# Attention by two head pairs per pipeline step, with the softmax sums' 1e-9 on GpSimd

## The chip, the cores and the metric

The kernel runs on one core of one Trainium2 chip. TensorE (PE) multiplies and transposes, VectorE (DVE), ScalarE (ACT) and GpSimd (POOL) work on vectors, and SyncE (SP) issues most of the DMAs. The metric is the device time of the core in microseconds (us), as the median of the runs shown.

## The reference

Three computations follow each other:

```
attention   q, k, v: 4 x 8 heads x 768 x 64; a key is kept if it is one of the first 8, or at most 95 behind
            scores = q k / 8 - slope[h] * distance, kept keys only; a = exp(scores - max)
            a = a / (sum(a) + 1e-9);  x = a v, as 3072 tokens x 512
experts     logits = x w_gate (512 x 8); each token goes to its best expert, with its softmax value as gate
            out = gate * (relu(x w1[e]) w2[e]),  w1 512 x 1024, w2 1024 x 512
feed-forward  h = out w_in (512 x 2048); g = (a0 + a1 h + a2 h^2 + a3 h^3) / (1 + |b0||h| + |b1| h^2 + 1e-6)
            result = g w_out (2048 x 512)
```

## The kernel before

Attention works on units: a unit is a tile of 128 tokens, 24 in all (4 sequences of NI = 6 tiles), and in each unit on NP = 4 pairs of heads. `seq` lists the 96 steps (u, hp), and the loop over t runs one step of it at a time as a software pipeline of four stages. Step t first issues stage D of step t-5, then A of step t, C of step t-3 and B of step t-1:

- A (stA, L586; stA2, L600 and L604): S = q k for the two heads of a pair, six products in two PSUM banks `sj` (q and k are split in two float32r parts, so three products a head). On VectorE a fused add and minimum takes the negated, masked scores to `nn` and their minimum `mn` (L600, shown as CUSTOM_DVE_ANT_0, and as ISA in the order). On ScalarE the exponential gives `pp` and its row sums `sm` (L604). A window has 232 keys, or 128 in a sequence's first tile.
- B (stB): four transpositions on TensorE (L616, `pt`), the 1e-9 added to the two sums on VectorE (L619, `rs`), `pt` copied to `pT` (on ScalarE for pair 1, L622, on VectorE for the others, L624), and the reciprocal of `rs` (L626).
- C (stC): four products with v (L638, in bank `ps_o`), a copy to `oT` on ScalarE (L641).
- D (stD): one product of `oT` with `iw`, which holds a unit matrix and the gate's weights (L647, in bank `ps_ox`). So x comes back with tokens on the partitions, and beside it the pair's part of the logits. VectorE multiplies both by `rs` (x L653, lw L657). After the last pair of a unit the logits are summed (lg, L666) and x is stored.

The same engines do other work in the loop. emit_tstep transposes q and k of later units (L512), copies them to `raw` on ScalarE (L520, L523, L524) and subtracts on GpSimd (L525), one half at a time. Every second unit from unit 5 on a block of expert 0's weights is loaded, and split a unit later: ScalarE rounds (L314), GpSimd subtracts (L315). Routing runs in small steps that wait in `filler`; each call of fill() between two larger operations emits one. Units are routed in groups of 4, 7, 6, 3, 3 and 1; a group's steps end with the sorted positions `pos` (L215), a store of the gates (L198) and one indirect DMA a unit on GpSimd that scatters token numbers to `tid` (L136, behind a memset, L135).

When all groups but the last two are routed, SyncE reads the numbers of expert 0's first 256 tokens back from DRAM (L128, `eidx`), and GpSimd gathers these tokens' rows of x (L250, `raw`). They form the early tile. Its products with expert 0's weights go in 64 small steps of three matmuls (L267 to L269), each step followed by work for ScalarE and VectorE (hh L293, hl L294). They fill what the attention leaves of TensorE at its end.

After the loop the string TAILS orders what is left: B, C and D with a number are these stages of the step that many from the end, G is the scaling of the gathered rows on VectorE (L254), X their transposition (L260), F with a number so many routing steps, E so many steps of the early tile. Then all engines meet a branch on `slow` (L821, L822; not taken here), TensorE counts the tokens (L1237), VectorE plans the experts' tiles (L1239 to L1378 and on), the early tile's remaining steps run, a second branch follows (L1445), and the experts begin. Each engine executes its own instructions in the order in which they are emitted.

## Time and profile before

| | us |
|---|---|
| median of 3 runs | 1171.92 |
| lowest and highest | 1169.7, 1175.31 |
| span of the profiled execution | 1169.0 |
| busy in it: PE, DVE, ACT, POOL | 1109.0, 954.6, 760.1, 434.6 |

The three runs lie around the span of the profiled execution, the median 2.9 us above it. Busy times of an engine overlap those of the others. The attention loop takes up roughly the first 265 us of the span, the tail and the first branch go to 289 us, the early tile's rest to 316 us, the experts and the feed-forward part to the end.

### The profile page before, as it was taken

Reading aid. Unit: us, or ns where it says so; the run is one execution under the profiler, and the core shown is the slowest. Engines: PE = TensorE matmul, PEld = TensorE weight load, DVE = VectorE, ACT = ScalarE, POOL = GpSimd, SP = SyncE. Lnnn points to the kernel's source line nnn. Section 1 sums busy time; section 2 is a strip of 40 time slices with the busy share of each in tenths; the row PEclk is TensorE's granted clock in tenths of the full one; section 3 lists DMA queues with packets and bytes.
Section 4 is the critical chain, followed back from the end, with each engine's and each line's share of the span. In section 5 each row is a group of like instructions: output and inputs, shape, how many; then the busy total and the mean of one; then the engine's idle time right before and its main releaser. Section 6 shows DMA issues by size and latency. Waiting matters only on the chain.

```text
span 1169.0 us, 19466 instructions
## 1 busy us (share of the span) xinstructions
PE 1109.0 (95%) x6636; PEld 982.8 (84%) x6636; DVE 954.6 (82%) x2200; ACT 760.1 (65%) x1695; POOL 434.6 (37%) x454
## 2 busy tenths in 40 slices
PE   8998988987699999999997999999999999999997
PEld 7876776766699888999996888999999999999996
DVE  7897878774667967887667999989898998989985
ACT  5886777662254555554555777777777777777774
POOL 4253444532422323132114535344342535344342
PEclk9998989798799999999999999999999999999999
DMA  9887787403477877887663000000100000000000
GB/s 177 186 132 162 164 94 173 87 20 105 114 226 251 302 243 248 283 302 269 211 204 123 1 27 28 28 28 1 46 10 28 28 27 28 19 27 10 1 28 27
DMA packets 122820, 130.65 MB, mean 112 GB/s; under 512 B 62799, under 2 KB 92671, under 8 KB 122704
## 3 DMA queue, kind: packets, MB, share of 16 engines
q1 hardware_dynamic: 108416, 99.78, 32.7%
q0 software_dynamic: 8624, 22.48, 5.6%
q10 hardware_dynamic: 5664, 6.98, 1.6%
q8 instruction: 56, 0.92, 0.4%
q14 instruction: 60, 0.49, 0.2%
HBM read 99.60 MB, written 29.61 MB: 111 GB/s over the span
## 4 chain that ended last, share of the span: by engine, by line
PE 59%; DVE 7%; ACT 2%; issue 2%; DMA 2%; POOL 1%; ACTq 0%; POOLq 0%; DVEq 0%; SPq 0%
PE acc L268 10%; PE acc L267 10%; PE acc L269 10%; PE ph L267 7%; PE ph L268 7%; PE ph L269 7%; PE ps_t L267 3%; PE ps_t L269 3%; PE ps_t L268 3%; DVE ta L1546 1%; DVE tcc L1545 1%; DVE ta L1595 1%; PE ps_t L260 1%; DVE tcc L1605 1%; DMA ysT<-y 1%
## 5 line engine op out<-in xcount | busy, mean ns | idle before, releaser
L1560 POOL TENSOR_TENSOR gl<-tcc,gh 128x384 fp32r<-128x384 f32 x127 | 128.9, 1015 | 293.8 <-ACT gh L1554 229.1
L267 PE MATMUL acc<-wa_h,gh 128*128 128x512 f32 x384 | 150.2, 391 | 5.9 <-ACT gh L1554 4.3
L269 PE MATMUL acc<-wa_h,gl 128*128 128x512 f32 x384 | 151.4, 394 | 1.7 <-POOL gl L1560 1.7
L268 PE MATMUL acc<-wa_l,gh 128*128 128x512 f32 x384 | 151.3, 394 | 0.0
L1545 DVE SCALAR_TENSOR_TENSOR tcc<-tcc,cf,tb 128x384 f32<-128x384 f32 x128 | 117.9, 921 | 13.7 <-DVE tcc L1605 0.5
L1596 ACT ACTIVATE tb<-ta,cf 128x384 f32<-128x384 f32 x128 | 79.0, 617 | 42.8 <-DVE ta L1595 32.8
L1595 DVE SCALAR_TENSOR_TENSOR ta<-ta,cf,tb 128x384 f32<-128x384 f32 x128 | 81.4, 636 | 31.0 <-ACT tb L1590 29.7
L604 ACT ACTIVATE pp<-nn,mn 128x232 f32<-128x232 f32 (+1 forms) x192 | 88.8, 465 | 26.6 <-DVE mn L600 23.5
L1546 DVE SCALAR_TENSOR_TENSOR ta<-ta,cf,tb 128x384 f32<-128x384 f32 x128 | 103.3, 807 | 0.0
L269 PEld LDWEIGHTS acc<-wa_h,gl 128*128 128x128 f32 x384 | 72.1, 188 | 20.0 <-POOL gl L1560 4.7
L267 PE MATMUL ph<-xh,wb_h 128*128 128x384 f32 (+3 forms) x252 | 86.8, 344 | 1.7 <-DVE tcc L1605 1.2
L267 PEld LDWEIGHTS acc<-wa_h,gh 128*128 128x128 f32 x384 | 72.1, 188 | 19.0 <-ACT gh L1554 5.7
L268 PE MATMUL ph<-xl,wb_h 128*128 128x384 f32 (+3 forms) x252 | 86.3, 343 | 0.3 <-DVE xl L953 0.2
L269 PE MATMUL ph<-xh,wb_l 128*128 128x384 f32 (+3 forms) x252 | 86.1, 342 | 0.0
L268 PEld LDWEIGHTS acc<-wa_l,gh 128*128 128x128 f32 x384 | 72.0, 188 | 11.4
L616 PE MATMUL pt<-ident,pp 128*116 128x128 f32 (+1 forms) x384 | 71.6, 311 | 2.3 <-ACT pp L604 2.3
L1589 ACT ACTIVATE ta<-ph 128x384 f32<-128x384 f32 x78 | 38.1, 488 | 54.0 <-PE ph L269 54.0
L600 DVE CUSTOM_DVE_ANT_0 nn<-sj,bm 128x232 f32<-128x232 f32 (+1 forms) x192 | 65.8, 373 | 6.8 <-PE sj L586 4.7
L1551 DVE SCALAR_TENSOR_TENSOR tcc<-ta,tcc 128x384 f32<-128x384 f32 x128 | 70.4, 550 | 0.0
L616 PEld LDWEIGHTS pt<-ident,pp 128*116 128x116 f32 (+1 forms) x384 | 49.3, 185 | 20.9 <-issue 15.3
L1554 ACT ACTIVATE gh<-tcc 128x384 fp32r<-128x384 f32 x128 | 65.1, 509 | 2.3 <-DVE tcc L1551 2.3
L1601 ACT ACTIVATE tb<-tb 128x384 f32<-128x384 f32 x128 | 65.1, 509 | 0.0
(335 smaller groups left out, 3352.9 us busy)
## 6 DMA issues: line engine op xcount, KB each, us to landing
wst<-in_moe_w_dram SPq DMA_DIRECT2D x72, 512.0 KB
wst<-in_moe_w_in_dram SPq DMA_DIRECT2D x16, 512.0 KB
wst<-in_moe_w_out_dram SPq DMA_DIRECT2D x16, 512.0 KB
xs<-x SPq DMA_DIRECT2D x24, 256.0 KB
hh<-in_v_dram SPq DMA_DIRECT2D x17, 256.0 KB
wf_in<-cv POOLq DMA_DIRECT2D x16, 256.0 KB
wf_out<-cv POOLq DMA_DIRECT2D x16, 256.0 KB
wst<-wf_in SPq DMA_DIRECT2D x8, 512.0 KB
```

The costliest lines, as they stand in the source:

```text
L267: nc.tensor.matmul(ps, lh, rh, start=first, stop=False)
L268: nc.tensor.matmul(ps, lh, rl, start=False, stop=False)
L269: nc.tensor.matmul(ps, ll, rh, start=False, stop=last)
L600: nc.vector.tensor_tensor_reduce(nn[:, 0:w], s2[j][:, 0:w], bmh, op0=ALU.add, op1=ALU.min, scale=1.0, scalar=3.0e38, accum_out=mn)
L604: nc.scalar.activation(pp[:, 0:w], nn[:, 0:w], AF.Exp, scale=-1.0, bias=mn, accum_out=sm[:, j:j + 1])
L616: nc.tensor.transpose(pt[0:w2, j, r, :], pv[:, r, :], ident)
L1545: nc.vector.scalar_tensor_tensor(pc_, pc_, na0, pb_, op0=ALU.add, op1=ALU.mult)
L1546: nc.vector.scalar_tensor_tensor(pa_, pa_, one, pb_, op0=ALU.add, op1=ALU.mult)
L1551: nc.vector.scalar_tensor_tensor(pc_, pa_, -2.0, pc_, op0=ALU.add, op1=ALU.mult)
L1560: eng.tensor_tensor(gl, prev[2], gh.bitcast(F32), op=ALU.subtract)
L1595: nc.vector.scalar_tensor_tensor(ta, ta, b1, tb, op0=ALU.mult, op1=ALU.add)
L1596: nc.scalar.activation(tb, ta, AF.Ln, bias=one)
```

## The change

A step of the pipeline now handles a group of HG = 2 pairs, so that a unit has two steps and the loop 48. The lags become 1 step for B, 2 for C and 3 for D. S of both pairs goes to the same two banks, the second pair 256 columns further on. The four transpositions, the products with v and the product with `iw` are issued for both pairs one after the other; `ps_o` and `ps_ox` hold both pairs, and one instruction each copies `oT` (256 columns), multiplies x (256) and lw (32). The reciprocal is taken once for four sums and moves to stage C; the 1e-9 is added on GpSimd, once for four sums. A step has 11 calls of fill() (before, 7), two halves of emit_tstep (one), and the warming products, mask pieces and TAILS are rewritten for 48 steps. Comments are gone, so lines of the attention part have other numbers after the change: S L588, the reduction L604, the exponential L608, the add L617, the transpositions L624, pT L631 and L633, C L647, oT L650, the reciprocal L651, D L659, x L667, lw L671, lg L680. In the diff, what builds the loads, stores and splits inside the loop is left out; they keep their conditions, with hg in place of hp.

```diff
-TAILS = "D5 G F1 C3 C2 B1 X0 C1 F3 D4 X1 D3 F3 F7 F1 E2 D2 F2 F1 E2 F2 F2 F1 F3 E1 F5 D1"
+TAILS = "D3 G F1 C2 B1 X0 C1 F3 D2 X1 F3 F7 F1 E2 D1 F2 F1 E2 F2 F2 F1 F3 E1 F5"
-WARM2 = 2, 2, 2, 4
+WARM2 = 4, 6
-MS = (7, 2, 4, 2)
+MS = (7, 2, 4, 4)
...
-        seq = [(u, hp) for u in range(units) for hp in range(NP)]
+        HG = 2
+        NG2 = NP // HG
+        seq = [(u, hg) for u in range(units) for hg in range(NG2)]
...
-        def stA(u, hp):
+        def stA(u, hg):
             bb, i = divmod(u, NI)
             w = P if i == 0 else WIN
-            s2 = []
             k1 = (i + 1) * GK
-            for j in range(2):
-                sj = psS.tile([P, 512], F32, name="sj")
-                s2.append(sj)
-            for n, (x, y) in enumerate(((0, 0), (0, 1), (1, 0))):
-                for j in range(2):
-                    hd = slice(j * D, (j + 1) * D)
-                    nc.tensor.matmul(s2[j][:, 0:w], qT[u][x][hd, hp, :], kr[hd, y, hp, k1 - w:k1], start=n == 0, stop=n == 2)
-            st[u, hp] = s2
-        def stA2(u, hp):
+            s2 = [psS.tile([P, 512], F32, name="sj") for j in range(2)]
+            for a in range(HG):
+                hp = HG * hg + a
+                for n, (x, y) in enumerate(((0, 0), (0, 1), (1, 0))):
+                    for j in range(2):
+                        hd = slice(j * D, (j + 1) * D)
+                        nc.tensor.matmul(s2[j][:, a * 256:a * 256 + w], qT[u][x][hd, hp, :], kr[hd, y, hp, k1 - w:k1],
+                                         start=n == 0, stop=n == 2)
+            st[u, hg] = s2
+        def stA2(u, hg):
             i = u % NI
             w = P if i == 0 else WIN
-            s2 = st[u, hp]
-            sm = wk.tile([P, 2], F32, name="sm", bufs=5)
-            pr = []
+            s2 = st[u, hg]
+            sm = wk.tile([P, HG, 2], F32, name="sm", bufs=4)
+            pr = {}
             for j in range(2):
-                h = 2 * hp + j
-                nn = wk.tile([P, WIN], F32, name=f"nn{j}")
-                mn = wk.tile([P, 1], F32, name=f"mn{j}")
-                bmh = bm[:, h, WIN:WB] if i == 0 else bm[:, h, 0:WIN]
-                nc.vector.tensor_tensor_reduce(nn[:, 0:w], s2[j][:, 0:w], bmh, op0=ALU.add, op1=ALU.min,
-                                               scale=1.0, scalar=3.0e38, accum_out=mn)
-                fill()
-                pp = wk.tile([P, WIN], F32, name=f"pp{j}")
-                nc.scalar.activation(pp[:, 0:w], nn[:, 0:w], AF.Exp, scale=-1.0, bias=mn, accum_out=sm[:, j:j + 1])
-                pr.append(pp)
-            st[u, hp] = [pr, sm]
-        def stB(u, hp):
+                for a in range(HG):
+                    h = 2 * (HG * hg + a) + j
+                    nn = wk.tile([P, WIN], F32, name="nn", bufs=4)
+                    mn = wk.tile([P, 1], F32, name="mn", bufs=6)
+                    bmh = bm[:, h, WIN:WB] if i == 0 else bm[:, h, 0:WIN]
+                    nc.vector.tensor_tensor_reduce(nn[:, 0:w], s2[j][:, a * 256:a * 256 + w], bmh, op0=ALU.add,
+                                                   op1=ALU.min, scale=1.0, scalar=3.0e38, accum_out=mn)
+                    fill()
+                    pp = wk.tile([P, WIN], F32, name=f"pp{a}{j}", bufs=2)
+                    nc.scalar.activation(pp[:, 0:w], nn[:, 0:w], AF.Exp, scale=-1.0, bias=mn, accum_out=sm[:, a, j:j + 1])
+                    pr[a, j] = pp
+            st[u, hg] = [pr, sm]
+        def stB(u, hg):
             i = u % NI
             w2 = P // 2 if i == 0 else HWIN
-            pr, sm = st[u, hp]
-            pt = psT.tile([P, 2, 2, P], F32, name="pt")
-            for j in range(2):
-                pv = pr[j][:, 0:2 * w2].rearrange("p (c r) -> p r c", r=2)
-                for r in range(2):
-                    nc.tensor.transpose(pt[0:w2, j, r, :], pv[:, r, :], ident)
-            pT = wk.tile([HWIN, 2, 2, P], F32, name="pT", bufs=3)
-            rs = wk.tile([P, 2], F32, name="rs", bufs=7)
-            nc.vector.tensor_scalar(rs, sm, 1e-9, None, op0=ALU.add)
-            fill()
-            if hp in ONACT:
-                nc.scalar.activation(pT[0:w2], pt[0:w2], AF.Copy)
-            else:
-                nc.vector.tensor_copy(pT[0:w2], pt[0:w2])
-            fill()
-            nc.vector.reciprocal(rs, rs)
-            fill()
-            st[u, hp] = [pT, rs]
-        def stC(u, hp):
+            pr, sm = st[u, hg]
+            rs = wk.tile([P, HG, 2], F32, name="rs", bufs=5)
+            nc.gpsimd.tensor_scalar(rs, sm, 1e-9, None, op0=ALU.add)
+            pts = []
+            for a in range(HG):
+                pt = psT.tile([P, 2, 2, P], F32, name="pt")
+                for j in range(2):
+                    pv = pr[a, j][:, 0:2 * w2].rearrange("p (c r) -> p r c", r=2)
+                    for r in range(2):
+                        nc.tensor.transpose(pt[0:w2, j, r, :], pv[:, r, :], ident)
+                pts.append(pt)
+            pTs = []
+            for a in range(HG):
+                pT = wk.tile([HWIN, 2, 2, P], F32, name="pT", bufs=3)
+                fill()
+                if HG * hg + a in ONACT:
+                    nc.scalar.activation(pT[0:w2], pts[a][0:w2], AF.Copy)
+                else:
+                    nc.vector.tensor_copy(pT[0:w2], pts[a][0:w2])
+                pTs.append(pT)
+                fill()
+            st[u, hg] = [pTs, rs]
+        def stC(u, hg):
             i = u % NI
             w2 = P // 2 if i == 0 else HWIN
-            pT, rs = st[u, hp]
+            pTs, rs = st[u, hg]
             vt = vts[u]
             ox = psM.tile([P, 512], F32, name="ps_o")
-            for r in range(2):
-                for j in range(2):
-                    nc.tensor.matmul(ox[j * D:(j + 1) * D, 0:P], vt[0:w2, 2 * hp + j, r, :], pT[0:w2, j, r, :],
-                                     start=(r == 0), stop=(r == 1))
-            oT = wk.tile([P, P], F32, name="oT", bufs=4)
-            nc.scalar.activation(oT, ox[:, 0:P], AF.Copy)
-            st[u, hp] = [oT, rs]
-        def stD(u, hp):
-            oT, rs = st.pop((u, hp))
+            for a in range(HG):
+                for r in range(2):
+                    for j in range(2):
+                        nc.tensor.matmul(ox[j * D:(j + 1) * D, a * P:(a + 1) * P], vt[0:w2, 2 * (HG * hg + a) + j, r, :],
+                                         pTs[a][0:w2, j, r, :], start=(r == 0), stop=(r == 1))
+            oT = wk.tile([P, HG, P], F32, name="oT", bufs=2)
+            nc.scalar.activation(oT, ox[:, 0:HG * P].rearrange("p (a q) -> p a q", a=HG), AF.Copy)
+            nc.vector.reciprocal(rs, rs)
+            st[u, hg] = [oT, rs]
+        def stD(u, hg):
+            oT, rs = st.pop((u, hg))
             ox = psM.tile([P, 512], F32, name="ps_ox")
-            nc.tensor.matmul(ox[:, 0:P + 2 * E], oT, iw[:, hp, :], start=True, stop=True)
-            if hp == 0:
+            OW = P + 2 * E
+            for a in range(HG):
+                nc.tensor.matmul(ox[:, a * OW:(a + 1) * OW], oT[:, a, :], iw[:, HG * hg + a, :], start=True, stop=True)
+            if hg == 0:
                 x = wk.tile([P, DM], F32, name="x", bufs=2)
                 lw = wk.tile([P, H, E], F32, name="lw", bufs=2)
                 xt[u] = (x, lw)
             x, lw = xt[u]
-            nc.vector.tensor_tensor(x[:, hp * P:(hp + 1) * P].rearrange("p (j d) -> p j d", j=2),
-                                    ox[:, 0:P].rearrange("p (j d) -> p j d", j=2),
-                                    rs.unsqueeze(2).to_broadcast([P, 2, D]), op=ALU.mult)
+            ov = ox[:, 0:HG * OW].rearrange("p (a c) -> p a c", a=HG)
+            xw = HG * P
+            nc.vector.tensor_tensor(x[:, hg * xw:(hg + 1) * xw].rearrange("p (a j d) -> p a j d", a=HG, j=2),
+                                    ov[:, :, 0:P].rearrange("p a (j d) -> p a j d", j=2),
+                                    rs.unsqueeze(3).to_broadcast([P, HG, 2, D]), op=ALU.mult)
             fill()
-            nc.vector.tensor_tensor(lw[:, 2 * hp:2 * hp + 2, :],
-                                    ox[:, P:P + 2 * E].rearrange("p (j e) -> p j e", j=2),
-                                    rs.unsqueeze(2).to_broadcast([P, 2, E]), op=ALU.mult)
-            if hp == NP - 1:
+            nc.vector.tensor_tensor(lw[:, 2 * HG * hg:2 * HG * (hg + 1), :].rearrange("p (a j) e -> p a j e", a=HG),
+                                    ov[:, :, P:OW].rearrange("p a (j e) -> p a j e", j=2),
+                                    rs.unsqueeze(3).to_broadcast([P, HG, 2, E]), op=ALU.mult)
+            if hg == NG2 - 1:
...
-            if 0 <= t - 5 < L:
-                stD(*seq[t - 5])
+            if t >= 3:
+                stD(*seq[t - 3])
-                stC(*seq[t - 3])
+            if t >= 2:
+                stC(*seq[t - 2])
...
-            if nxt:
-                emit_tstep(*nxt.pop(0))
+            for _ in range(3 if t == 0 else 2):
+                if nxt:
+                    emit_tstep(*nxt.pop(0))
...
             fill(True)
+            fill(True)
```

TensorE in one step in the middle of the loop, in the order of issue, before; `sj` are the scores' banks, `pt` the transposed probabilities:

```order
L647 MATMUL ps_ox<-iw,oT 128x144
L586 MATMUL sj<-kr,qh 128x232 x4
L586 MATMUL sj<-kr,ql 128x232 x2
L638 MATMUL ps_o<-pT,hh 64x128 x4
L616 MATMUL pt<-ident,pp_1755 116x128 x2
L616 MATMUL pt<-ident,pp_1760 116x128 x2
L512 MATMUL ps_qk<-ident,hl 128x128 x2
```

and after:

```order
L659 MATMUL ps_ox<-iw,oT 128x144 x2
L588 MATMUL sj<-kr,qh 128x232 x4
L588 MATMUL sj<-kr,ql 128x232 x2
L588 MATMUL sj<-kr,qh 128x232 x4
L588 MATMUL sj<-kr,ql 128x232 x2
L647 MATMUL ps_o<-pT,hh 64x128 x8
L624 MATMUL pt<-ident,pp_1666 116x128 x2
L624 MATMUL pt<-ident,pp_1676 116x128 x2
L624 MATMUL pt<-ident,pp_1671 116x128 x2
L624 MATMUL pt<-ident,pp_1681 116x128 x2
L512 MATMUL ps_qk<-ident,xh 128x128 x4
```

The five kinds of products that followed each other once for each pair now follow once for two pairs, each with twice the number.

GpSimd near the end of the loop, before; `kr` and `ql` are the low parts of k and q, `tid` the scattered token numbers, `raw` the gathered rows:

```order
L525 TENSOR_TENSOR kr<-raw,kr 128x4x128
L525 TENSOR_TENSOR ql<-raw,qh 128x512
L198 DMA xs<-g_4620 128x3x16
L525 TENSOR_TENSOR kr<-raw,kr 128x4x128
L135 MEMSET nop 1x1
L136 DMA tid<-tok,pos 24704x1
L135 MEMSET nop 1x1
L136 DMA tid<-tok,pos 24704x1
L135 MEMSET nop 1x1
L136 DMA tid<-tok,pos 24704x1
L525 TENSOR_TENSOR ql<-raw,qh 128x512
L250 DMA raw<-xs,eidx 128x528 x2
```

and after:

```order
L617 TENSOR_SCALAR rs<-sm 128x4
L198 DMA xs<-g_4293 128x3x16
L617 TENSOR_SCALAR rs<-sm 128x4
L135 MEMSET nop 1x1
L136 DMA tid<-tok,pos 24704x1
L135 MEMSET nop 1x1
L136 DMA tid<-tok,pos 24704x1
L135 MEMSET nop 1x1
L136 DMA tid<-tok,pos 24704x1
L617 TENSOR_SCALAR rs<-sm 128x4
L250 DMA raw<-xs,eidx 128x528 x2
L617 TENSOR_SCALAR rs<-sm 128x4
```

The three scatters of tiles 17 to 19 stood between subtractions of q and k, which the loop issues for later units; they now come behind the last of these, between the adds of the last steps, and the add of the last step comes behind the two gathers.

VectorE just ahead of the first branch (its last two rows), before; `hl` is the low part of the early tile's hidden values, `pos` the last tile's position:

```order
L294 SCALAR_TENSOR_TENSOR hl<-sj,hh 128x256
L206 TENSOR_TENSOR rr<-sj,oh 128x8
L190 TENSOR_SCALAR se<-se 128x1
L209 TENSOR_SCALAR em_5146<-em_5146 128x1
L193 RECIPROCAL gate<-se 128x1
L294 SCALAR_TENSOR_TENSOR hl<-sj,hh 128x256
L212 TENSOR_REDUCE rank<-rr 128x1
L197 COPY g_5204<-gate 128x16
L215 TENSOR_TENSOR pos<-em_5146,rank 128x1
L294 SCALAR_TENSOR_TENSOR hl<-sj,hh 128x256 x2
L821 TENSOR_LOAD slow
L822 COMPARE_AND_BRANCH
```

and after:

```order
L206 TENSOR_TENSOR rr<-sj,oh 128x8
L190 TENSOR_SCALAR se<-se 128x1
L209 TENSOR_SCALAR em_4553<-em_4553 128x1
L294 SCALAR_TENSOR_TENSOR hl<-sj,hh 128x256
L193 RECIPROCAL gate<-se 128x1
L212 TENSOR_REDUCE rank<-rr 128x1
L197 COPY g_4578<-gate 128x16
L215 TENSOR_TENSOR pos<-em_4553,rank 128x1
L294 SCALAR_TENSOR_TENSOR hl<-sj,hh 128x256
L834 TENSOR_LOAD slow
L835 COMPARE_AND_BRANCH
```

Of the six rows that write `hl` ahead of the branch, two are left, and the rest comes behind the branch.

## Rows read from the trace of the kernel before

**Rows 1.** The top of the page: span, busy time of each engine.

```profile
span 1169.0 us, 19466 instructions
...
PE 1109.0 (95%) x6636; PEld 982.8 (84%) x6636; DVE 954.6 (82%) x2200; ACT 760.1 (65%) x1695; POOL 434.6 (37%) x454
```

**Rows 2.** Windows: stretch, us, busy PE, PEld, DVE, ACT, POOL; granted clock, DMA share, GB/s.

```profile
23.00:92.00 69.00, 64.31 (x639) 51.40 (x638) 58.79 (x287) 54.73 (x183) 26.64 (x25) 1.00 0.88 164
92.00:102.00 10.00, 9.40 (x62) 7.25 (x63) 7.92 (x35) 6.78 (x22) 4.28 (x3) 0.66 1.19 240
...
282.00:318.00 36.00, 19.39 (x127) 19.00 (x127) 18.31 (x65) 6.61 (x13) 10.17 (x8) 0.76 0.35 85
...
318.00:1169.00 851.00, 833.52 (x4264) 759.94 (x4264) 711.51 (x1080) 561.04 (x1059) 307.64 (x301) 1.00 0.31 105
```

**Rows 3.** Timeline of TensorE, one pair step: start us, us, engine, line, tiles.

```profile
42.57 0.41 PE L647 MATMUL ps_ox<-iw,oT 128*128 128x144 f32 x2
...
42.91 0.49 PE L586 MATMUL sj<-kr,qh 64*128 64x232 f32 x4
...
43.43 0.66 PE L638 MATMUL ps_o<-pT,hh 116*64 116x128 f32 x8
...
44.02 0.70 PE L616 MATMUL pt<-ident,pp 128*116 128x128 f32 x4
...
44.78 0.41 PE L647 MATMUL ps_ox<-iw,oT 128*128 128x144 f32 x2
```

**Rows 4.** Timeline of TensorE, windows that cut the merged rows of the same step.

```profile
43.12 0.27 PE L586 MATMUL sj<-kr,qh 64*128 64x232 f32 x2
...
43.81 0.28 PE L638 MATMUL ps_o<-pT,hh 116*64 116x128 f32 x2
```

**Rows 5.** Timeline of TensorE: first S products of pair 6 and of pair 94.

```profile
22.98 0.48 PE L586 MATMUL sj<-kr,qh 64*128 64x232 f32 x4
...
260.44 0.49 PE L586 MATMUL sj<-kr,qh 64*128 64x232 f32 x4
```

**Rows 6.** Waits, 92 to 102 us: engine line <- releaser, us, times, longest.

```profile
DVE x L653 <- DMA xs<-x: 3.7, 1, 3.7
```

**Rows 7.** The add: its durations ns min/median/max; its group at 23 to 263 us.

```profile
L619 DVE TENSOR_SCALAR rs<-sm x96: 115/164/2454, 15.8 to 267.9; 128x2 f32<-128x2 f32 x96
...
L619 DVE TENSOR_SCALAR rs<-sm 128x2 f32<-128x2 f32 x90 | 44.9, 499 | 0.0
```

**Rows 8.** Timeline of VectorE at 40 and 199 us.

```profile
40.10 1.13 DVE L619 TENSOR_SCALAR rs<-sm 128x2 f32<-128x2 f32 x1
...
199.06 2.31 DVE L184 TENSOR_TENSOR cum<-cum,oh 128x8 bf16<-128x8 bf16 x1
```

**Rows 9.** Timeline of GpSimd at 40 and 199 us.

```profile
39.93 1.28 POOL L525 TENSOR_TENSOR kr<-raw,kr 128x512 fp32r<-128x512 f32 x1 [2.66 <-ACT kr L524]
...
199.01 2.35 POOL L315 TENSOR_TENSOR wa_l<-wst,wa_h 128x1024 fp32r<-128x1024 f32 x1 [1.75 <-ACT wa_h L314]
```

**Rows 10.** Timeline of GpSimd, 240 to 296 us.

```profile
250.42 0.96 POOL L136 DMA_INDIRECT tid<-tok,pos  x1 [0.22 <-issue]
...
262.48 0.98 POOL L250 DMA_INDIRECT raw<-xs,eidx  x1 [9.68 <-issue]
...
281.10 0.98 POOL L136 DMA_INDIRECT tid<-tok,pos  x1 [0.22 <-issue]
```

**Rows 11.** Waits of SP's queue, 250 to 300 us.

```profile
SPq L128 <- DMA tid<-tok,pos: 10.2, 1, 10.2
```

**Rows 12.** Timeline of VectorE in the tail and behind the branch.

```profile
266.99 0.87 DVE L254 TENSOR_SCALAR raw<-raw 128x512 f32<-128x512 f32 x2
...
296.20 6.77 DVE L1378 SCALAR_TENSOR_TENSOR svals<-tot,redo 128x1 int32<-128x1 f32 x1
```

**Rows 13.** Timeline of TensorE: early tile, and the first expert product.

```profile
303.35 0.58 PE L268 MATMUL ph<-hl,wa_h 128*128 128x256 f32 x1 [7.68 <-DVE hl L294]
...
317.86 0.47 PE L267 MATMUL ph<-wa_h,cv 128*128 128x512 f32 x1 [2.10 <-ACT nop L1445]
```

56 lines of the change are left out of this document (26 added, 30 removed).

## The prediction

> **What bounds the kernel now.** I began with the page's top [rows 1]: one core, a span of 1169.0 us, TensorE busy 95% of it. An average like that hides stages, so next came the windows [rows 2]. From 318 us to the end TensorE is busy 833.52 of 851 us: the expert and feed-forward products fill it, the change touches nothing there, and that part only shifts. All that the change can move lies before 318 us: the attention loop (to about 265 us), a tail, a branch and the early tile of expert 0. In the stretch 23 to 92 us TensorE is busy 64.31 of 69 us, VectorE 58.79, ScalarE 54.73.
>
> Then the timeline of TensorE inside one undisturbed pair step [rows 3]: the product of stage D starts at 42.57 and again at 44.78 us, 2.21 us later, with no idle time named in between. TensorE sets the step. But it does not stream all that time. Cutting the window inside the merged rows [rows 4] shows single starts: products of one shape follow each other after about 0.11 us, and at a change of shape more time goes by. D's two slots from 42.57 to the first S product at 42.91 take 0.34, 0.12 over; 42.91 to the second S slot at 43.12 is 0.21; from there to C at 43.43 is 0.31 for two slots, so 0.20 in the last; C's first slot has 0.05 more than 0.11 (43.43 to 43.81 for three); the last C at 43.81 to the first transposition at 44.02 is 0.21; and the six 128x128 products from 44.02 to 44.78 take 0.76, 0.10 more than six times 0.11. The excesses 0.12, 0.10, 0.09, 0.05, 0.10 and 0.10 make 0.56 us a step that is spent on changing over.
>
> The loop as a whole is slower than its step. Pair 6 starts S at 22.98, pair 94 at 260.44 [rows 5]: 237.5 us for 88 steps, against 88 x 2.21 = 194.5. The missing 43 us I divided by walking the gaps between S starts and asking what each gap's last wait was: about 18 us hang on DMA, the first and largest at 92 us, where VectorE waits 3.7 us for a store of x to drain and TensorE's products for it in turn [rows 6]; about 25 us hang on bursts of VectorE and the half-speed stretch that follows one of them. What feeds those bursts is in rows 7: the 1e-9 add, 128x2 elements, takes 0.164 us in the median and 2.454 at most, 44.9 us over 90 of them, so about 30 us more than 90 x 0.164. The long ones lie under GpSimd work: 1.13 us at 40.10 [rows 8] while GpSimd runs its 1.28 us subtraction from 39.93 [rows 9].
>
> The Trainium skill, "SBUF — State Buffer", section "SBUF: two separate sides", says that VectorE and GpSimd share one port pair as an exclusive lock. The trace agrees with it: the add ends as the GpSimd subtraction does. By that page the routing's steps with two SBUF inputs stay exposed after the change, and rows 8 and 9 show one, 2.31 us at 199.06 under GpSimd's weight split from 199.01. By the page the sum below stays as it is; were the lock only the add's, it would be 6 us lower.
>
> **The change, part by part.** *Grouping.* Streaming stays; the changes of shape come once for two pairs. A group step has the floor 2 x 2.21 - 0.56 = 3.86 us for TensorE in place of 4.42. ScalarE is next: 54.73 us over some 30 pairs [rows 2] is 1.8 us a pair, 3.6 a group, and one merged copy of o saves under 0.1; VectorE, less some 10 us of the adds' excess in that stretch (a third of 30), has 1.63 a pair and, without the adds themselves, 3.1 a group. Three engines at 80 to 95% of 3.86 don't run at the floor. I take 3.97; bounds are 3.86 and 4.42 (nothing gained). 44 groups at 3.97 are 175 us.
>
> *Lag.* D runs three group steps behind A, where it was five pair steps, and C two where it was three; in time the lags grow from 11.1 to 11.9 us and 6.6 to 7.9. So chains have as much time as before and I cost it at zero. Two pairs in one bank means that the first reduction waits until the second pair's products of that bank are there as well, about 0.5 us later. The cover is VectorE's own slack, 3.86 less 3.1; if routing steps fill that, each such group loses up to 0.5. The Trainium skill, "PSUM — Partial Sum Buffer", section "PSUM bank collisions raise a hardware error", forbids an engine to read a bank while TensorE writes it, which would make this wait hard. No run here shows a collision; by the page the sum stays, as the 0.5 is counted.
>
> *The add and the reciprocal.* 96 adds leave VectorE: 96 x 0.164 at most (they overlap their neighbours in part), plus the 30 us of excess. 48 adds of 128x4 come to GpSimd. The trace has no such operation there; its nearest rows are VectorE's own add, at least 0.115 us [rows 7], and GpSimd's 1.28 us for a 128x512 subtraction [rows 9], I take 0.2 for its size, 10 us in all on an engine that is 37% busy [rows 1]. It can be late, though: it stands behind the subtractions and, every fourth step, behind the weight split of 2.35 us. The reciprocal that waits for it is emitted a group step later, so it has some 3.9 us; I cost it at zero, with 0 and 2 us for each of some ten splits and scatters as bounds.
>
> *Stalls after.* Most of VectorE's 25 us go; the routing's own exposure stays, I leave 6. The DMA's 18 us don't go: they come where loads, stores and the scatters of token numbers fall together, the DMA share stands at 1.19 at 92 to 102 us [rows 2], and a faster loop asks for the same bytes sooner. I take 22, bounds 14 and 35. So the last group step starts at about 23 + 175 + 6 + 22 = 226 us, where the last two pairs began at 260.44: 34 us gained, bounds 20 and 44.
>
> *The tail.* Here the change costs. Routing steps are dealt out by fill() slots, 28 a unit before and 22 now, so the group of tiles 17 to 19 gets its positions later in the loop. Before, its third scatter started at 250.42, 10 us ahead of pair 94. Now its three scatters stand behind the add of group 45, in the last group step. What follows has a fixed length: SP waits 10.2 us for the scattered numbers [rows 11], GpSimd gathers the early tile's rows from 262.48 [rows 10], VectorE scales them at 266.99 [rows 12]. From the end of the third scatter (251.4) to that is 15.6 us; before, the loop's last steps covered all of it, and VectorE reached the scaling without waiting. Now the scatters end about 2.8 us into the last group step, the scaling comes at 226 + 2.8 + 15.6 = 244.4, VectorE reaches it some 5 us into that step, and everything queued behind it there (the last copies of pT, x and the last routing) stands for 13 us. The add of the last group also stands behind both gathers. From the scaling to the end of the last scatter it was 15.1 us (to 282.1, rows 10); with D only twice and fewer early products in between I take 13.5. The last scatter then ends 32 us after the last group step's start, before it was 21.6 after pair 94's. Loss: 10 us, bounds 4 and 14.
>
> *Behind the branch.* Before the branch 8 steps of the early tile's products are emitted in place of 24; the order shows two rows that write hl there where six stood. The 16 steps go behind the branch. TensorE spends 19.39 us on some 42 steps in 282 to 318 us [rows 2], 0.46 each at the mixed clock (0.76): 16 x 0.46 = 7 us later. The 7.68 us that TensorE waits at 303.35 [rows 13], behind one VectorE operation of 6.77 us at 296.20 [rows 12], I leave as they are. Bounds: 0 (the branch comes sooner relative to the landing of the scatters, and the waiting is used) and 12. Loss 7.
>
> *Warm-up and masks:* as many warming products as before (10), masks at the same pace in time; zero.
>
> Sum: 34 - 10 - 7 = 17 us less than the profiled 1169.0, so 1152. The median of the runs shown is 1171.92, 2.9 above that span; I carry these 2.9 over and forecast 1155.
>
> **The rivals.** *The tail eats it (slower or equal).* One mechanism: the three scatters of tiles 17 to 19 in the last group step, with GpSimd's queue and the 15.6 us chain in front of the scaling, then the clock at half speed when TensorE starts again. At their upper ends the two late terms are 14 + 12 = 26, and if half speed lasts over the tail's products another 5: 31 us. It decides where the loop gains less than that; with a loop gain of 20 to 25 the time is 1178 to 1183. For it: the chain is fixed in length and had no slack beyond those 10 us. Against: the loop's gain is the sum of two independent ones.
> *DMA bounds the loop.* Gains in the stretches 66 to 102 and 143 to 186 us are nil and the rest is split between ScalarE and DMA; loop gain 17 to 20, net 0 to 5: about 1169. For: DMA share 0.88 already at 23 to 92 us [rows 2]. Against: TensorE runs without idle time over pairs 6 to 22 at that share.
> *The reciprocal waits for GpSimd.* Its in-order queue puts the add behind splits that wait for ScalarE and DMA; VectorE stands for it, and steps go to 4.4 or more where weights are split, ten times 2 to 4 us. Net gain some 0 to 8 us less than forecast, 1155 to 1165. For: the add stands behind the split in GpSimd's order. Against: the lag of a whole step.
> *The tail is covered.* Should the tail's waits overlap with what the branch waits for anyway, the late terms are 6 and not 17, and with the loop at its floor (44 groups at 3.86) the time is 1138 to 1142.
>
> **How the numbers follow.** Forecast 0.45 (1146 to 1163), tail covered 0.17, late reciprocal 0.12, DMA-bound 0.13, tail eats it 0.13. About 0.5%, 5.9 us, is what a measurement of this kernel tells from no change: 1166 to 1178. Faster: the first three whole but for 0.02, and little of the fourth, 0.74. Same: most of the DMA case and the near edge of the last, 0.14. Slower: the rest, 0.12. The range 1136 to 1176 leaves out the far end of the covered tail and of the last rival. The forecast's own is 1146 to 1163.
>
> **What would show it.** The step: S starts 3.9 to 4.0 us apart in a calm stretch; 4.4 would fell the first term. The adds: none on VectorE, and its reciprocal not over 0.2 us by itself; a wait of VectorE for GpSimd before it would show the third rival. The tail: the scaling of the gathered rows behind a wait of 10 us or more on VectorE, some 18 us after the last S. The branch: over 50 early products' steps behind it. The prediction is wrong if the last S does not start before 240 us, or if the distance from there to the first expert product, 57.4 us before (260.44 to 317.86, rows 5 and 13), does not grow to about 75.

## The result, and the profile after

| | before | after |
|---|---|---|
| median of 13 runs each | 1175.12 us | 1162.77 us |
| lowest and highest | 1169.7, 1179.99 | 1157.2, 1172.41 |
| ratio, 95% interval | | 0.9901, 0.9875 to 0.9926 |
| span of the profiled execution | 1169.0 | 1161.0 |

The change makes the kernel about 1% faster, some 12 us; it was forecast at 17 us less than the three runs shown, whose median lies 3.2 us under that of the 13. The two profiled executions differ by 8.0 us, less than the medians do, because that of before lay near the lower end of its kernel's runs. What follows from the two traces is reckoned against these 8 us.

The top of the page after, beside [rows 1]:

```profile
span 1161.0 us, 19304 instructions
...
PE 1081.2 (93%) x6636; PEld 979.4 (84%) x6636; DVE 914.0 (79%) x1960; ACT 752.6 (65%) x1647; POOL 448.5 (39%) x502
```

TensorE has 28 us less to be busy for with the same 6636 matmuls, VectorE 41 less. The stretches of the trace (start and end, length, busy time of PE, PEld, DVE, ACT, POOL, granted clock, DMA share, GB/s):

```profile
23.00:80.00 57.00, 55.46 (x618) 48.40 (x617) 51.55 (x220) 51.70 (x169) 28.89 (x38) 1.00 0.92 183
80.00:97.00 17.00, 11.19 (x92) 9.59 (x92) 6.36 (x29) 9.38 (x29) 5.46 (x6) 0.80 0.97 157
...
222.00:262.00 40.00, 18.46 (x125) 15.60 (x124) 13.62 (x66) 6.57 (x22) 12.07 (x22) 0.66 0.24 69
262.00:310.00 48.00, 26.15 (x175) 25.72 (x176) 15.18 (x68) 7.86 (x16) 10.52 (x7) 0.72 0.26 64
...
318.00:1161.00 843.00, 826.01 (x4234) 754.84 (x4232) 705.28 (x1073) 557.43 (x1054) 303.27 (x298) 1.00 0.32 104
```

Up to 80 us TensorE is busy 97% of the time, where [rows 2] had 93% in about the same stretch. From 80 to 97 us a stall stands out, and from 222 to 310 us TensorE is busy half of the time, at two thirds of the clock. The first expert product comes at 309.54 us, 851.5 us ahead of the end; before it was 317.86 and 851.1. So the part behind it only shifted, as the prediction had it.

One group step on TensorE, the rows that answer to [rows 3] and [rows 4]:

```profile
42.85 0.66 PE L659 MATMUL ps_ox<-iw,oT 128*128 128x144 f32 x4
43.44 0.49 PE L588 MATMUL sj<-kr,qh 64*128 64x232 f32 x4
43.76 0.27 PE L588 MATMUL sj<-kr,ql 64*128 64x232 f32 x2
43.88 0.39 PE L588 MATMUL sj<-kr,qh 64*128 64x232 f32 x4
44.10 0.27 PE L588 MATMUL sj<-kr,ql 64*128 64x232 f32 x2
44.30 1.09 PE L647 MATMUL ps_o<-pT,hh 116*64 116x128 f32 x16
45.33 1.14 PE L624 MATMUL pt<-ident,pp 128*116 128x128 f32 x8
46.30 0.60 PE L512 MATMUL ps_qk<-ident,hl 128*128 128x128 f32 x4
46.74 0.66 PE L659 MATMUL ps_ox<-iw,oT 128*128 128x144 f32 x4
```

From D at 42.85 to D at 46.74 it is 3.89 us for two pairs. Each kind of product has twice the starts of a pair step and only one change of shape. The second `qh` group follows the first `ql` group after 0.12 us, as products of one shape do: going from one pair to the next costs nothing more.

The add, now on GpSimd, and VectorE's waits in the loop (waiter, releaser, us in total, times, longest):

```profile
L617 POOL TENSOR_SCALAR rs<-sm x48: 211/223/273, 17.3 to 240.9; 128x4 f32<-128x4 f32 x48
```

```profile
DVE x L667 <- DMA xs<-x: 13.7, 2, 8.6
...
DVE rs L651 <- POOL rs L617: 1.2, 2, 0.8
```

It takes 0.223 us on GpSimd (0.2 was the estimate), and its reciprocal is hardly ever waited for: 1.2 us in all. The 13.7 us for stores of x are now the largest wait of VectorE in the loop.

The tail, which answers to [rows 10 to 12]. GpSimd:

```profile
225.62 0.97 POOL L136 DMA_INDIRECT tid<-tok,pos  x1 [0.22 <-issue]
226.66 0.22 POOL L617 TENSOR_SCALAR rs<-sm 128x4 f32<-128x4 f32 x1
238.47 1.04 POOL L250 DMA_INDIRECT raw<-xs,eidx  x1 [11.60 <-issue]
239.82 0.97 POOL L250 DMA_INDIRECT raw<-xs,eidx  x1 [0.30 <-issue]
240.85 0.22 POOL L617 TENSOR_SCALAR rs<-sm 128x4 f32<-128x4 f32 x1
...
258.55 1.00 POOL L136 DMA_INDIRECT tid<-tok,pos  x1 [0.22 <-issue]
```

SyncE's wait for the scattered numbers and its read of them, and VectorE's scaling of the gathered rows:

```profile
SPq L128 <- DMA tid<-tok,pos: 15.3, 1, 15.3
```

```profile
235.31 0.38 SPq L128 DMA_DIRECT2D eidx<-tid  x1
```

```profile
243.98 0.49 DVE L254 TENSOR_SCALAR raw<-raw 128x512 f32<-128x512 f32 x1 [17.64 <-DMA raw<-xs,eidx]
```

Between the third scatter's end (226.59) and the scaling it is 17.4 us, and VectorE stood idle for 17.64 us up to the scaling. Before, no idle time stood in front of that row. Of the 17.4 us, 8.7 pass until SyncE issues the read at 235.31 (the scatter lands 9.6 us after its start, just ahead of that), 3.2 until the gather and 5.5 until the scaling; the rest of SyncE's 15.3 us lies ahead of the scatter's end. And behind the branch, beside [rows 12, 13], VectorE with a step of the plan and the writes of `hl`, then TensorE:

```profile
281.34 2.71 DVE L1306 CAST fi<-sidx 128x24 f32<-128x24 int32 x1 [5.96 <-DMA sidx<-tid]
...
290.89 1.08 DVE L294 SCALAR_TENSOR_TENSOR hl<-ph,hh 128x256 fp32r<-128x256 f32 x3
```

```profile
291.36 0.58 PE L267 MATMUL ph<-xh,wa_h 128*128 128x256 f32 x1 [13.60 <-DVE hl L294]
...
309.54 0.47 PE L267 MATMUL ph<-wa_h,cv 128*128 128x512 f32 x1 [2.10 <-ACT nop L1458]
```

The wait for `hl` is 13.6 us in place of 7.68, and the rows of VectorE show why: the plan waits 5.96 us for numbers read back from DRAM, and these writes of `hl` come behind its end.

### The profile page after: what moved, and what is told of

Read it like the earlier page. It is cut to its first block, busy times and chain, and to the rows that moved or that the text cites. A ratio compares the mean times of both kernels' runs of the same rounds, so it can differ in the third digit from the quotient of the medians.

```text
span 1161.0 us, 19304 instructions
## 1 busy us (share of the span) xinstructions
PE 1081.2 (93%) x6636; PEld 979.4 (84%) x6636; DVE 914.0 (79%) x1960; ACT 752.6 (65%) x1647; POOL 448.5 (39%) x502
## 4 chain that ended last, share of the span: by engine, by line
PE 62%; DVE 7%; DMA 2%; issue 1%; ACT 1%; POOL 0%; POOLq 0%; ACTq 0%; DVEq 0%; SPq 0%
PE acc L268 10%; PE acc L267 10%; PE acc L269 10%; PE ph L267 8%; PE ph L269 8%; PE ph L268 8%; PE ps_t L267 3%; PE ps_t L269 3%; PE ps_t L268 3%; DVE ta L1559 1%; DVE tcc L1558 1%; DMA wst<-wf_out 1%; DVE ta L1608 1%; PE ps_t L260 1%; DVE tcc L1618 1%
## 5 line engine op out<-in xcount | busy, mean ns | idle before, releaser
L1558 DVE SCALAR_TENSOR_TENSOR tcc<-tcc,cf,tb 128x384 f32<-128x384 f32 x128 | 118.3, 924 | 13.7 <-ACT xh L965 0.5
L608 ACT ACTIVATE pp<-nn,mn 128x232 f32<-128x232 f32 (+1 forms) x192 | 88.4, 463 | 17.7 <-DVE mn L604 17.5
L604 DVE CUSTOM_DVE_ANT_0 nn<-sj,bm 128x232 f32<-128x232 f32 (+1 forms) x192 | 63.5, 372 | 8.1 <-PE sj L588 5.0
L267 PE MATMUL ph<-xh,wa_h 128*128 128x464 f32 (+3 forms) x152 | 54.1, 356 | 14.5 <-DVE hl L294 13.6
L624 PE MATMUL pt<-ident,pp 128*116 128x128 f32 (+1 forms) x384 | 57.3, 295 | 0.0
```

Of the source, the lines that this page charges most:

```text
L267: nc.tensor.matmul(ps, lh, rh, start=first, stop=False)
L608: nc.scalar.activation(pp[:, 0:w], nn[:, 0:w], AF.Exp, scale=-1.0, bias=mn, accum_out=sm[:, a, j:j + 1])
L1558: nc.vector.scalar_tensor_tensor(pc_, pc_, na0, pb_, op0=ALU.add, op1=ALU.mult)
```

## The experiments

Each ratio is against the kernel before, in runs on the same chip beside it; the interval is of 95%. The quoted expectations call the kernels e1 to e11; the label stands with each. The changed kernel was measured twice, which gives the measure: 0.9901 (0.9875 to 0.9926), and 0.9922 (0.9894 to 0.9951) the second time.

> The changed kernel itself once more, beside the others of this call, as their measure: 0.988 to 0.993 of the kernel before.

So differences below 0.4% between kernels that were not measured side by side are not told apart here. Single traces spread more. The loop of the changed kernel stands unaltered in three of them (two of this kernel, one of e3), and its last S starts at 221.95, 225.56 and 218.74 us; the loop of e1 and e5 is one and the same, and its last S starts at 219.04 and 226.41. A last S that comes some 7 us earlier or later in one trace therefore shows nothing by itself.

**The add back on VectorE** (e1).

```diff
-            nc.gpsimd.tensor_scalar(rs, sm, 1e-9, None, op0=ALU.add)
+            nc.vector.tensor_scalar(rs, sm, 1e-9, None, op0=ALU.add)
```

> The changed kernel with the 1e-9 back on VectorE, one add of 128x4 a group, the reciprocal left in stage C. Theory (the add costs VectorE by lying under GpSimd's subtractions): of 48 adds about half last 1 to 2.4 us, some 25 us in sum, and with 3.1 us of other work in a step of 3.89 the steps of the routing and of the weight splits get late; the last S starts 2 to 6 us after the changed kernel's 221.95, the whole is 2 to 6 us longer. Rival (VectorE has slack enough once the steps are grouped, so the move to GpSimd does nothing): the last S at 220 to 224 and the time within 2 us of the changed kernel.

Measured: 0.9922 (0.9896 to 0.9949), no difference to the changed kernel. Its adds are stretched, to 25.7 us in sum as expected, though 9 of the 48 last over 1 us and not half of them:

```profile
L617 DVE TENSOR_SCALAR rs<-sm x48: 142/399/3247, 18.5 to 240.6; 128x4 f32<-128x4 f32 x48
```

(ns min, median, max.) Yet the last S starts at 219.04, no later than in the traces of the changed kernel. The longest add falls into group step 15 (counted from 1), which takes 7.06 us; but where the stall that follows ends, S starts at 90.59, beside 90.65 in the changed kernel. The rival holds: the stretched adds cost no time that the runs show, although VectorE is busy 55.39 of the 57 us from 23 to 80 (the changed kernel: 51.55). So the change gives without the add's move all that it gives with it.

**The add alone** (e2). The kernel before, the reciprocal moved to stage C as well.

```diff
-            nc.vector.tensor_scalar(rs, sm, 1e-9, None, op0=ALU.add)
+            nc.gpsimd.tensor_scalar(rs, sm, 1e-9, None, op0=ALU.add)
...
-            nc.vector.reciprocal(rs, rs)
             fill()
             st[u, hp] = [pT, rs]
...
             nc.scalar.activation(oT, ox[:, 0:P], AF.Copy)
+            nc.vector.reciprocal(rs, rs)
```

> The kernel before, steps of one pair, with the add on GpSimd and the reciprocal moved to stage C, nothing else. Theory (two effects in the change, the grouping worth 0.53 us a pair of steps and the add's excess on VectorE worth the bursts): the calm step stays at 2.21 us, no add on VectorE, the last pair but one starts S some 8 to 15 us before 260.44, the whole is 8 to 14 us faster than the kernel before. Rival (the bursts come from routing, DMA and clock, not from the adds): the loop's end moves by less than 4 us. Second rival (GpSimd's queue makes the add late): the reciprocal waits and steps of 2.5 us and more appear, slower than before.

Measured: 0.9993 (0.9969 to 1.0017), no change. But the loop was ahead: the S that started at 256.11 before starts at 243.35, 12.8 us sooner, with the step still at 2.21. Then VectorE stands. Its row, and GpSimd's:

```profile
242.22 0.27 DVE L666 TENSOR_REDUCE lg<-lw 128x8 f32<-128x64 f32 x1
252.18 0.17 DVE L641 RECIPROCAL rs<-rs 128x2 f32<-128x2 f32 x1 [9.70 <-POOL rs L619]
```

```profile
249.54 1.04 POOL L250 DMA_INDIRECT raw<-xs,eidx  x1 [9.13 <-issue]
250.88 0.98 POOL L250 DMA_INDIRECT raw<-xs,eidx  x1 [0.30 <-issue]
251.93 0.80 POOL L619 TENSOR_SCALAR rs<-sm 128x2 f32<-128x2 f32 x3
```

The reciprocal waits 9.70 us for an add that is queued behind the two gathers, which wait for the scattered numbers. So a faster loop and this wait stand against each other. How much of the 12.8 us is the adds' doing, this trace doesn't tell: the next kernel has the same loop up to unit 22, and its lead at this S is 6.1 us, with 7 us more of stall at pairs 65 to 67.

**The same, without that wait** (e7): the add on VectorE in the last two units.

```diff
-            nc.gpsimd.tensor_scalar(rs, sm, 1e-9, None, op0=ALU.add)
+            (nc.vector if u >= 22 else nc.gpsimd).tensor_scalar(rs, sm, 1e-9, None, op0=ALU.add)
```

> The kernel before, steps of one pair, the add on GpSimd for the first 22 units and on VectorE for the last two, the reciprocal in stage C. Theory (in e2 the loop had gained 12.8 us by pair 93 and lost 9.7 of them when VectorE waited for adds behind the two gathers): without that wait the gain stays, 9 to 13 us faster than the kernel before, 0.989 to 0.992, step still 2.21. Rival (the loop's gain is given back by the scatters' fixed way to the scaling whatever the adds do): VectorE waits ahead of the scaling instead, and the time is within 4 us of the kernel before.

Measured: 0.9939 (0.9914 to 0.9964), about 7 us faster, a little under the theory's range. The same S starts at 249.99, and VectorE now waits 3.3 us ahead of the scaling, so a part goes the rival's way. For steps of one pair the adds on VectorE are a real cost, then (4 to 10 us by the interval, the reciprocal's later place included, which no run parts from it); for steps of two they are not.

**D of the last group at the end again** (e3), so that early products go beside the last routing steps, ahead of the branch.

```diff
-TAILS = "D3 G F1 C2 B1 X0 C1 F3 D2 X1 F3 F7 F1 E2 D1 F2 F1 E2 F2 F2 F1 F3 E1 F5"
+TAILS = "D3 G F1 C2 B1 X0 C1 F3 D2 X1 F3 F7 F1 E2 F2 F1 E2 F2 F2 F1 F3 E1 F5 D1"
```

> The changed kernel with D of the last group at the end of TAILS again, where it stood before; six writes of hl ahead of the branch in place of two. Theory (the 13.6 us that TensorE waits at 291 come from early products that were left for behind the branch, where hl stands behind the whole plan on VectorE): that wait falls under 4 us, the way from the last scatter's end to the first expert product is 36 to 42 us in place of 50.0, the last scatter ends 4 to 7 us later, the whole is 4 to 9 us faster than the changed kernel. Rival (the way behind the branch is set by the landing of the scatters and the two reads of sidx): the wait only moves, the time stays within 2 us.

Measured: 0.9816 (0.979 to 0.9843), about 10 us faster than the changed kernel. TensorE's waits between the last scatter and the experts:

```profile
264.31 0.17 PE L1250 MATMUL ps_t<-cums,ones 128*128 128x8 bf16 x1 [6.37 <-DVEq L835]
...
279.84 1.11 PE L260 MATMUL ps_t<-ident,xrow 128*128 128x128 f32 x4 [4.09 <-DVE xrow L254]
...
289.61 0.47 PE L267 MATMUL ph<-wa_h,cv 128*128 128x512 f32 x1 [2.23 <-PEq L1428]
```

The wait for `hl` is gone; what is left is 4.09 us for the next tile's rows. From the last scatter's end (258.30) to the first expert product it is 31.3 us in place of 50.0, better than the theory expected and less than the 35.8 of before. The last scatter ends 39.6 us behind the last S, 2 us later than in the changed kernel's trace. The traces of two different times make the gain too large, 19.9 us up to the first expert product; e1's, taken beside this one, has that product at 302.05, 12.4 us later, which agrees with the 10 us of the ratios. So the order in TAILS, and not the faster loop, made the way behind the branch long.

**Routing earlier** (e4): the early tile from 18 tiles, the gathers held back. EWAIT is the number of empty fill slots between the read of the scattered numbers and the gathers.

```diff
-        groups = [4, 7, 6, 3, 3, 1]
+        groups = [4, 7, 4, 3, 5, 1]
-EWAIT = 6
+EWAIT = 45
```

> The changed kernel with groups of 4, 7, 4, 3, 5 and 1 tiles in place of 4, 7, 6, 3, 3 and 1 and EWAIT 45 in place of 6, so that the early tile takes its rows from the first 18 tiles, whose scatters stand four group steps earlier on GpSimd, and the gathers at the place in its order where they were. Theory (the 17.6 us that VectorE waits ahead of the scaling are the fixed way from the scatters to the gathered rows, uncovered): the wait falls to under 5 us, the scaling comes 12 to 16 us earlier against the last S, two more scatters and a longer routing in the tail give 3 us back, the whole is 8 to 13 us faster than the changed kernel. Rival (the gather waits for DMA traffic of the loop's end or for GpSimd's queue, whatever the scatters' place): the wait stays over 10 us, the time within 3 us.

Measured: 0.9893 (0.9873 to 0.9912). The scaling came at 234.19, only 4.4 us behind the last S (22.0 in the changed kernel). But the last S came at 229.82, 7.9 us later than in the changed kernel's first trace and 11.1 later than in e3's, taken beside it. SyncE stands 24.4 us for the scattered numbers, and the store of x that is queued behind its read goes out only at 218.95; VectorE waits 5.69 us for a store of x up to 222.53. (The two adds behind the gathers, at 230.86, come after that S.) The wait ahead of the scaling went as the theory has it, the gain is mostly given back; the time is the rival's, though not for the rival's reason.

**Both remedies, with the add on VectorE** (e5). The edits of e1 and e3 together:

> The changed kernel with the add back on VectorE and D of the last group last in TAILS. Theory (the early products ahead of the branch are worth 8 to 10 us, and with the add off GpSimd nothing of the last steps stands behind its gathers, worth 0 to 3): 9 to 13 us faster than the changed kernel, 0.978 to 0.982 of the kernel before. Rival (the add's place matters in the loop after all): no better than e3's 0.9816, or worse by 2 us and more.

Measured: 0.9772 (0.9744 to 0.9801), 1.5% less than the changed kernel beside it, some 18 us where the theory had 9 to 13; against e3's 0.9816 the two intervals overlap. And with tiles 11 to 16 scattered more densely, so that the next group's routing starts sooner (e6):

```diff
-                                       ROOM if gi + 3 < len(groups) else 0))
+                                       (ROOM, ROOM, 2, 0, 0, 0)[gi]))
```

> e5 with 2 empty slots in place of 10 behind each scatter of tiles 11 to 16, so that the routing of tiles 17 to 19 no longer waits behind them and its scatters stand two group steps earlier in GpSimd's order. Theory (VectorE's wait ahead of the scaling is the fixed way from these scatters): the wait falls by about 7 us from the 17 it has, three quarters of it come back in the time, 4 to 7 us faster than e5. Rival (the denser scatters slow the loads of the loop, as in e4, and the last S comes later by as much): within 2 us of e5.

Measured: 0.9737 (0.9713 to 0.9761), on the theory's side by its centre, though the intervals overlap. VectorE waits 4.57 us ahead of the scaling, in place of 17.38; the last S comes 5.6 us later than in e5's trace, which is within what traces of one loop differ by.

**Where the loop's stalls come from** (e8). The scatters of the first four tiles are put behind those of the next seven, and there without the ten empty slots between them.

```diff
+                    if gi == 0:
+                        held = [z for z in steps[-gn * (1 + ROOM):] if z is not None]
+                        steps = steps[:-gn * (1 + ROOM)]
+                        lgrp["held"] = held
+                    elif gi == 1:
+                        steps = steps + lgrp.pop("held")
```

> The changed kernel with the scatters of the first four tiles (65 to 78 us in its trace) put behind those of tiles 4 to 10. Theory (the loop's remaining stalls are the loads and stores that the scatters slow: while they run the DMA moves 71 to 144 GB/s in place of 190 and more, and 12 us later VectorE waits 8.6 us for a store of x): the stalls of group steps 18 and 19, 10.5 and 6.15 us long, fall to under 5 us each, and new ones of several us come behind the later scatters, at group steps 36 to 42; the last S within 6 us either way of the changed kernel's. Rival (the loop's loads are too much for the DMA by themselves from 50 us on): steps 18 and 19 stay as long.

Measured: 0.9917 (0.9887 to 0.9946), unchanged. Two stretches of its trace, then the second of them in the changed kernel, in the columns of the stretches of the result:

```profile
80.00:97.00 17.00, 17.00 (x196) 15.09 (x193) 15.30 (x63) 16.73 (x51) 9.57 (x10) 1.00 0.76 170
...
150.00:195.00 45.00, 28.53 (x254) 24.56 (x254) 24.06 (x108) 23.45 (x72) 19.53 (x25) 0.73 0.80 126
```

```profile
150.00:195.00 45.00, 40.22 (x390) 34.36 (x388) 31.98 (x139) 33.52 (x106) 24.42 (x30) 0.89 0.99 162
```

VectorE's waits for stores of x from 150 to 195 us, in the trace of e8:

```profile
DVE x L667 <- DMA xs<-x: 21.3, 2, 11.3
```

In 80 to 97 us TensorE is busy throughout, where it was 11.19 us; the group steps 18 and 19 take 3.89 us each. The stalls appear where the scatters went: in 150 to 195 us TensorE has 28.53 us (the changed kernel 40.22), VectorE waits 21.3 us for stores of x there, and the steps 34 and 38 take 11.95 and 15.78 us. The last S is at 224.78. The rival falls: with the loads alone, no group step from the fourth to the 25th takes over 4.73 us.

**Further on that way** (e9, with e6's edits). More fill slots at the end of the loop, and the last q's subtraction on VectorE:

```diff
-EWAIT = 6
+EWAIT = 20
...
-                (nc.vector if u < SUBV else nc.gpsimd).tensor_tensor(ql, raw, qh.bitcast(F32), op=ALU.subtract)
+                (nc.vector if u < SUBV or (u == B * NI - 1 and nm == "qn") else nc.gpsimd).tensor_tensor(ql, raw, qh.bitcast(F32), op=ALU.subtract)
...
-            fill(True)
-            fill(True)
+            for _ in range(5 if t >= 41 else 2):
+                fill(True)
```

> e6 with the last q's subtraction on VectorE, 14 fill slots a group step from step 41 on in place of 11, EWAIT 20 in place of 6. Theory (the scatters of tiles 17 to 19 set the scaling, and a subtraction that stands behind them held the last S for 5 us): scatters one group step earlier, scaling 2 to 4 us earlier, 1 to 4 us faster than e6. Rival (VectorE is full in these steps and each routing step makes them longer): no difference to e6, within 2 us.

Measured: 0.9722 (0.9689 to 0.9754). VectorE waits 1.18 us ahead of the scaling, but the scaling itself comes at 241.19, as in e6's trace (240.97): not told apart from it. With one tile less ahead of the gathers (e10; 11 fill slots again, EWAIT 28):

```diff
-        groups = [4, 7, 6, 3, 3, 1]
+        groups = [4, 7, 5, 3, 4, 1]
```

> e6 with groups of 4, 7, 5, 3, 4 and 1 tiles, so that the early tile takes its rows from the first 19, the last q's subtraction on VectorE, EWAIT 28. Theory (one tile less ahead of the gathers moves the scatters some 8 us forward, so that VectorE does not wait ahead of the scaling at all): the wait is gone, 3 to 6 us faster than e6. Rival (as in e4 the scatters then fall on loads of the loop, and the last S is later by what the scaling gains): within 2 us of e6.

Measured: 0.972 (0.9685 to 0.9754). No wait ahead of the scaling at all, and the last S at 235.62, 3.2 us later than in e9's trace: by its time the rival's outcome, though so small a difference of the last S shows nothing. Last (e11), the kernel with more fill slots and three buffers for x in place of two, three for nn in place of four:

```diff
-                    nn = wk.tile([P, WIN], F32, name="nn", bufs=4)
+                    nn = wk.tile([P, WIN], F32, name="nn", bufs=3)
...
-                x = wk.tile([P, DM], F32, name="x", bufs=2)
+                x = wk.tile([P, DM], F32, name="x", bufs=3)
```

> e9 with three buffers for x in place of two, and three for nn in place of four to make room. Theory (behind each run of scatters VectorE waits 7.9 to 12.9 us for the store of a unit's x to drain, because the buffer is needed again two units later, and a third buffer gives it one unit, 7.8 us, more): those waits fall by 5 us and more each, the last S comes 8 to 16 us earlier, and half of it or less comes back in the time, since the scatters of tiles 17 to 19 and the branch follow; 3 to 10 us faster than e9. Rival (the weights' and inputs' loads are as late as the stores, so the next wait takes over): the stalls move to ScalarE's wait for weights or TensorE's for q and k, the last S within 4 us of e9's 232.4 and the time within 2 us.

Measured: 0.9763 (0.9723 to 0.9803), no gain. VectorE no longer waits for stores. The two waits that stand in their place at 80 to 98 us:

```profile
DVE nn L604 <- ACT pp L608: 7.6, 3, 6.6
ACT wa_h L314 <- DMA wst<-in_moe_w_dram: 5.4, 1, 5.4
```

The load of weights is just as late, and ScalarE's wait for it now holds VectorE through `pp`. But over the whole loop VectorE waits 39.3 us in 32 places for `pp`, that is for ScalarE to be done with a buffer of nn; in e9's trace it does so nowhere. The smaller nn pool is a rival that this edit doesn't part from the theory's, so whether a third buffer for x is worth something stays open.

The best two kernels of the series are about 2.8% faster than the kernel before, where the change alone has 1%.

## Why the prediction was right, and where it was not

The direction, the time (1162.77, 0.2 us inside the upper end of the forecast's own 1146 to 1163) and the mechanism of most terms came out. The sizes of three terms did not: the loop gave 4.5 us more than forecast, the two late terms took 13.2 more. In the traces 8.3 of the 17 us are left, in the medians 12.4. That the time still lies in the range is luck in part.

*The step.* Forecast 3.97 us with a floor of 3.86; the trace has 3.88 to 3.89 wherever nothing stalls. The floor was read right from the changes of shape. The 0.1 us for three engines so near their limits was not needed: ScalarE is busy 51.70 of 57 us at 23 to 80 us and still keeps up. VectorE's 3.1 us a group was too low: its 51.55 of 57 us make 3.5, so it had 0.4 us of slack a step in place of 0.8, and the step held.

*The stalls.* Forecast 28 us, 22 of DMA and 6 of VectorE. From 22.69 to the last S at 221.95 it is 199.3 us, less 44 steps of 3.885: 28.3, of which some 19 in steps behind scatters (last section). Step and stalls together put the last S 38.5 us ahead of 260.44; 34 was the forecast. A slip in counting stood in it: the S at 22.98 belongs to pair 5 (counted from 0, as pair 94 is), so 89 steps and not 88 lie up to 260.44, and the loop before lost 41 us to stalls, not 43.

*What the stalls are.* That DMA's part stays was right, and the moved scatters show what sets it off. The part of VectorE was put down to the adds. That they cost the kernel before some 7 us is shown by the adds moved alone; but in the changed kernel the grouping takes that cost away without the move, as the first experiment shows. The prediction counted the move as needed. The stalls fell by 12.5 us in all; what took the other 5 is not traced.

*The tail.* Forecast 10 us lost with bounds of 4 and 14, measured 16.0: from the last group's S to the last scatter's end it is 37.6 us, before 21.6. This term is the first mis-sized one. The scatters ended 4.6 us into the last step and not 2.8, the fixed way to the scaling took 17.4 us and not 15.6, and what follows took 15.6 and not 13.5. The way is less fixed than the word says: it takes 15.1 to 17.5 us in the eight traces in which VectorE waits for its end and EWAIT is 6. For what follows the prediction had counted on fewer products. TensorE, behind an idle time of 15.97 us, runs 60 matmuls at a granted clock of 0.50, where before it ran 112 at 1.00 in 15.1 us. But the clock isn't what sets the stretch: in e1's trace 60 run at 0.80, and it takes 15.4 us.

*Behind the branch.* Forecast 7 us lost with bounds of 0 and 12, measured 14.2: 50.0 us from the last scatter's end to the first expert product, before 35.8. The step that failed is "16 x 0.46", products counted as time on TensorE, with the wait of 7.68 us left as it was. What happens is a wait: the writes of `hl` stand on VectorE behind the whole plan, with the plan's own wait in it. Products that have not been run ahead of the branch can't run there for want of `hl`; TensorE is out of work for 13.6 us. The experiment e3 shows that the order in TAILS is the cause. The distance from the last S to the first expert product, which was to grow from 57.4 to about 75 us, grew to 87.6.

*The rivals.* That the tail eats the gain came nearest: the two late terms were 30 us, close to its 31, and only the larger gain of the loop kept the change on the faster side. That DMA bounds the loop to a gain of 17 to 20 us fell (38.5), and so did the covered tail: the waits are there. The late reciprocal was not seen in the changed kernel (1.2 us), but it is real where the gathers come ahead of several adds, as the add alone shows with 9.70 us. Its price was mis-added in the prediction: ten waits of 2 to 4 us make 20 to 40 us, not a net gain that is 0 to 8 us less. The Trainium skill, "SBUF — State Buffer", section "SBUF: two separate sides", has VectorE and GpSimd share a port pair as an exclusive lock; the adds on VectorE in the first experiment agree: the shortest takes 0.142 us, and the longest, 3.247 us from 66.44 on, ends as a subtraction and a weight split end that GpSimd runs one behind the other from 66.05 to 69.65.

Open: why TensorE's wait at the branch is 5.6 to 14.1 us from kernel to kernel, why the scatter ahead of the scaling needs 9.6 us to land, and what sets the 15.6 us from the scaling to the last scatter's end.

## What to carry to other kernels

Where small matmuls of several shapes alternate, count the starts at the changes of shape: 0.56 us of each step went into changing, and doing two steps' worth of each shape in one go saved every second of these changes. A faster loop uncovers chains of fixed length that its end had covered, so steps dealt out by loop position have to be dealt out anew: here the ends cost 30 of 38 us. And a load taken off an engine by one edit may be free already by another; try them apart.
